# One block's k by a transposing load, its v on another queue, and PSUM copies placed by a table, in a two-layer H3 and SwiGLU kernel

## The chip, the cores and the metric

The kernel runs on one core of one Trainium2 chip. A core has five engines that run their own instruction streams and meet at semaphores: TensorE (PE in the profile; its weight loads are listed as PEld), VectorE (DVE), ScalarE (ACT), GpSimd (POOL) and SyncE (SP). DMAs are started by instructions on SP's and ACT's queues and carried out by 16 DMA engines. The metric is the device time of one execution in microseconds (us), lower is better.

## The reference

All arrays are bf16. Two equal layers run over x, a sequence of S = 2048 rows of D = 512 channels; the MLP has F = 1792 hidden channels. Both layers use the same q, k, v, filters and weights. Cut to what matters:

```python
def A(q, k, v, shift_k, ssm_k, ssm_D):            # H3: here q is LN(x)
    k_shift = sum(pad(k)[t:t+S] * shift_k[:, 3-t] for t in range(4))   # 4 taps per channel
    kv = k_shift * v
    y = irfft(rfft(kv, 2*S) * rfft(ssm_k, 2*S))[:S]    # causal convolution along S, per channel
    return q * (y + kv * ssm_D)
def B(x, w_gate, w_up, w_down):
    return (silu(x @ w_gate) * (x @ w_up)) @ w_down
x = A_q
for _ in range(2):
    x = x + A(layernorm(x), k, v, shift_k, ssm_k, ssm_D)
    x = x + B(layernorm(x), w_gate, w_up, w_down)
```

`k`, `v`, `shift_k`, `ssm_k` and `ssm_D` do not depend on x, so the convolution's result y is needed once and serves both layers.

## The kernel before, in words

**The convolution.** The 2048 rows are cut into four blocks of 512. Each block of kv and of the filter h (`ssm_k`) is turned into a spectrum by matmuls with cosine and sine tables (`fwd`), the spectra of two blocks are multiplied elementwise on DVE (`X` of kv by `G`/`H` of the filter, into `Z`), and matmuls with the transposed tables (`inv`) bring the products back (`Y`). The tables are made on the chip: iota on POOL, phases `ph` on DVE, Sin on ACT; `inv` is `fwd` through a transposing DMA. D is added to row 0 of the filter, once: `drow` is cleared by DVE, filled by a small DMA, and added by DVE when row 0 of h is copied out of PSUM (`transpose_h`, L479, the add at L502).

**The taps.** kv needs k shifted by 0 to 3 rows and scaled per channel. That is a matmul of k, transposed to channels by rows (`kTb`), against diagonal matrices `dg`: the identity times one tap, 16 of them (4 groups of channels by 4 taps). The taps come as `tapR`, are turned by PE into `tapF`, and the diagonals are made on DVE, ACT and POOL (L1188 and L1192). The result in PSUM is multiplied by v into `vt` (L536 for block 0).

**The first k.** For blocks 1 to 3, `kTb` is loaded by a transposing DMA (L366). For block 0 (`K0 = "rows"`) the rows are loaded plainly as `kn` (L364), `transpose_k` (L369 to L387) transposes them by 16 PE instructions (L378), and four copies bring them out of PSUM, two on ACT (L384) and two on DVE (L386).

**The FFN.** There are 16 units: layer by block by half a block of 256 rows. The normed rows are transposed to `zT`; gate and up projections go to PSUM tiles `pf` (matmuls of 256 columns, at the helper's line L323), Silu of the gate on ACT gives `sg` (L974), a copy of the up projection gives `ht` (L977, ACT), DVE multiplies them (L979), and the down projection goes to `pd` (L994), copied out as `dn` (L1075, ACT) and added to x. The layer norm's 1/sqrt is a power on POOL (`rstd`, L826, or L855 where ACT made the sums).

**The order of the work.** Every operation is recorded by `Plan.add` with an engine, a cost, the buffers it reads and writes, and perhaps a latency. `Plan.order` then sorts all operations by one table, `ORDER`, which was searched off the chip with these costs: `PW` and `PWA` are the costs of the two powers, `SAME` and `CROSS` the gaps between dependent operations of one or two engines. It gives PSUM slots (rings `pf` of 4, `pc` of 2, `pd` of 2) in that order, and each engine's instructions are issued in it. So the costs have no effect at run time except through the order and the slots. `Plan.issue` fills long planned gaps of PE before 32 us with dummy matmuls (`warm`, L1304).

**The queues at the start.** SP starts the loads of h of block 0 (`hn`), k, v, x (`xc`), h and v of block 1, the gate weights, then the two inverse tables, k of block 1, the up weights and the down weights. ACT's queue starts the taps and `drow`. PE runs 27 dummy matmuls, the taps' transposes, 16 transposes of h, then h spectrum and k transposes in turn, the 64 tap matmuls with h spectrum between, and from 13.6 us the spectrum of kv.

The lines that say what a sentence can't:

```python
def load_v(b, due=None, after=()):
    vt[b] = new("y" if b == 1 else "v", "vt", [P, R, D], parts=R)
    if b == 0 and K0 == "dma":
        return add("ACT", 0.45, lambda: nc.scalar.dma_start(out=vt[b].t[:], in_=v_t[:, b]), w=[vt[b]], lat=5.5, due=-69.5, after=[h0])
    return add("SP", 0.6, lambda: nc.sync.dma_start(out=vt[b].t[:], in_=v_t[:, b]), w=[vt[b]], ...)
```

Of the kernel before, what the change touches and what calls it, by code (L numbers as in the profile page):

```python
# [9 lines left out]
P = 128  # L10
# [13 lines left out]
PW = 1.2  # L24
# [15 lines left out]
DGE = 'DDAP'  # L40
# [3 lines left out]
PWA = 2.4  # L44
EVEN = True
SUMS = False
K0 = "rows"
CK0, LT0 = 3.0, 3.5
# [5 lines left out]
SHARE = {(1, 0, 1): 2, (0, 2, 0): 2, (1, 3, 0): 2}  # L54
ORDER = [
# [79 lines left out]


class Op:
    __slots__ = ("eng", "cost", "lat", "emit", "bufs", "preds", "succs", "due", "fixed", "conv", "grp", "dest", "sl", "end", "start", "n")


class Plan:
# [1199 lines left out]
```

## Time and profile before

| what | before |
|---|---|
| time, median of 3 runs (range) | 343.24 us (342.78 to 343.31) |
| the profiled execution: span, and with the 2.1 us around it | 341.1 us, 343.2 us |
| PE busy, matmuls | 336.9 us, 2563 |
| DVE busy, instructions | 282.4 us, 478 |
| ACT busy, instructions | 252.5 us, 496 |
| POOL busy, instructions | 37.3 us, 46 |
| share of PE in the chain that ended last | 94% |

How to read the profile. The span runs from the first to the last instruction of one profiled execution. The page gives busy time per engine, the span in 40 slices with the busy share of each in tenths, the chain of work that ended last, and groups of instructions by line. A row of a group is: line, engine, operation, output<-input, shapes, count | busy us, mean ns | idle us before them and what ended it. A row of the timeline is: start, duration, engine, line, operation, output<-input, shapes, count. A row of the chain is start, duration and what ran. The rows of the DMA view give KB of each and the median us from the issue to the landing; q1 is SP's queue there and q10 ACT's. Durations of a row of several matmuls include the last one's passage through the array.

### The profile page before, as it was taken

The numbers are of one execution on the slowest core, as the hardware profiler recorded it, in microseconds if no ns is written. First come the engines' busy times: TensorE is split into PE (matmuls) and PEld (weight loads), VectorE is DVE, ScalarE is ACT, GpSimd is POOL, SyncE is SP. The second block draws the span as 40 slices with busy tenths as digits, with TensorE's granted clock in tenths as the row PEclk, the third lists the DMA queues.
The fourth block names the chain that finished last, engine by engine and source line by source line (L and its number), as shares of the span: only waits on it lengthen the run. The fifth ranks groups of instructions, "written<-read, shape, count | busy, mean of one in ns | idle before, by whom it ended". The sixth has DMA issues, their size and how long they took to land.

```text
span 341.1 us, 6468 instructions
## 1 busy us (share of the span) xinstructions
PE 336.9 (99%) x2563; PEld 242.8 (71%) x2563; DVE 282.4 (83%) x478; ACT 252.5 (74%) x496; POOL 37.3 (11%) x46
## 2 busy tenths in 40 slices
PE   8999999999999999999999999999999999999996
PEld 7657858678687567768587756768685877777683
DVE  8899999999999999999999999889997533726022
ACT  7899999999977475778999973768665545545451
POOL 4000100002106100103100100101101000001000
PEclk9999999999999999999999999999999999999999
DMA  7999314050224175010110224010101110001111
GB/s 280 333 320 341 52 31 63 0 156 1 34 46 94 31 102 164 3 30 2 33 20 13 48 46 125 0 33 1 33 0 44 36 33 0 17 16 21 27 33 31
DMA packets 42088, 22.95 MB, mean 67 GB/s; under 512 B 33989, under 2 KB 39882, under 8 KB 42058
## 3 DMA queue, kind: packets, MB, share of 16 engines
q1 hardware_dynamic: 41904, 22.49, 26.0%
q8 instruction: 20, 0.33, 0.4%
q14 instruction: 10, 0.08, 0.1%
q10 hardware_dynamic: 154, 0.05, 0.1%
HBM read 12.33 MB, written 2.10 MB: 42 GB/s over the span
## 4 chain that ended last, share of the span: by engine, by line
PE 94%; ACT 3%; DMA 1%; SPq 0%; issue 0%; ACTq 0%
PE pf L323 57%; PE pd L994 28%; PE ps L323 6%; PE ps L470 2%; DMA kn<-in_A_k_dram 1%; ACT H L431 1%; ACT Yk L729 1%; ACT ks L526 0%; ACT n L874 0%; PE pt L378 0%; PE pt L489 0%; ACT zT L940 0%; ACT X L431 0%; SPq L354 0%; ACT xc L1052 0%
## 5 line engine op out<-in xcount | busy, mean ns | idle before, releaser
L323 PE MATMUL pf<-zT,wg_sb 128*128 128x256 bf16 (+1 forms) x872 | 110.3, 276 | 0.0
L323 PE MATMUL pf<-zT,wu_sb 128*128 128x256 bf16 (+1 forms) x872 | 110.0, 275 | 0.1
L994 PE MATMUL pd<-wd_sb,ht 128*128 128x512 bf16 (+1 forms) x462 | 106.2, 373 | 0.0
L323 PEld LDWEIGHTS <-wu_sb 128*128 128x128 bf16 x872 | 85.3, 98 | 18.9 <-issue 0.6
L323 PEld LDWEIGHTS <-wg_sb 128*128 128x128 bf16 x872 | 85.3, 98 | 17.3
L977 ACT CAST ht<-pf 128x512 bf16<-128x512 f32 x112 | 65.0, 592 | 23.0 <-PE pf L323 22.8
L974 ACT ACTIVATE sg<-pf 128x512 bf16<-128x512 f32 x112 | 66.6, 606 | 20.8 <-PE pf L323 17.3
L994 PEld LDWEIGHTS <-ht 128*128 128x128 bf16 x462 | 45.0, 98 | 44.1
L979 DVE TENSOR_TENSOR ht<-ht,sg 128x1024 bf16<-128x1024 bf16 (+1 forms) x61 | 38.9, 642 | 19.8 <-ACT ht L977 13.7
L826 POOL TENSOR_TENSOR rstd<-ve,nhalf 128x2 f32<-128x2 f32 x24 | 25.1, 1047 | 192.6 <-DVE ve L824 192.6
L821 DVE BATCH_NORM_STATS2 bnst<-xc 128x6 f32<-128x512 bf16 x48 | 31.8, 684 | 0.5
L1075 ACT CAST dn<-pd 128x512 bf16<-128x512 f32 x30 | 17.2, 590 | 17.5 <-PE pd L994 17.5
L431 ACT ACTIVATE X<-ps 128x512 bf16<-128x512 f32 x32 | 18.9, 606 | 10.5 <-PE ps L323 10.0
L1078 DVE TENSOR_TENSOR xc<-xc,dn 128x1024 bf16<-128x1024 bf16 x15 | 10.3, 687 | 16.8 <-ACT dn L1075 16.8
L669 DVE TENSOR_TENSOR t<-X,G 128x2048 bf16<-128x2048 bf16 x18 | 21.9, 1218 | 0.1
L665 DVE TENSOR_TENSOR t<-X,G 128x2048 bf16<-128x2048 bf16 x18 | 21.9, 1219 | 0.0
L855 POOL TENSOR_TENSOR rstd<-ve,nhalf 128x2 f32<-128x2 f32 x8 | 8.4, 1052 | 78.5 <-ACT ve L853 78.5
L679 DVE TENSOR_TENSOR Z<-Z,t 128x2048 bf16<-128x2048 bf16 x12 | 14.7, 1221 | 0.3
L677 DVE TENSOR_TENSOR t<-t,t 128x2048 bf16<-128x2048 bf16 x12 | 14.6, 1220 | 0.2
L431 ACT ACTIVATE H<-ps 128x512 bf16<-128x512 f32 x24 | 14.2, 612 | 0.0
L901 DVE TENSOR_TENSOR n<-n,Yk 128x1024 bf16<-128x1024 bf16 x15 | 10.3, 690 | 3.1 <-ACT n L874 1.9
L323 PE MATMUL ps<-hs,fwd 128*128 128x512 bf16 x40 | 12.7, 379 | 0.1
(103 smaller groups left out, 321.8 us busy)
## 6 DMA issues: line engine op xcount, KB each, us to landing
hn<-in_A_ssm_k_dram SPq DMA_DIRECT2D x4, 512.0 KB, 5.5
vt<-in_A_v_dram SPq DMA_DIRECT2D x4, 512.0 KB, 5.6
xc<-in_A_q_dram SPq DMA_DIRECT2D x4, 512.0 KB, 4.9
out_dram<-xc SPq DMA_DIRECT2D x15, 128.0 KB, 1.8
wg_sb<-in_B_w_gate_dram SPq DMA_DIRECT2D x1, 1792.0 KB
wu_sb<-in_B_w_up_dram SPq DMA_DIRECT2D x1, 1792.0 KB, 8.0
wd_sb<-in_B_w_down_dram SPq DMA_DIRECT2D x1, 1280.0 KB, 11.6
kn<-in_A_k_dram SPq DMA_DIRECT2D x1, 512.0 KB, 4.3
```

The costliest lines, as they stand in the source:

```text
L323: nc.tensor.matmul(o, lhsT=lhsT, rhs=rhs, start=(n == 0), stop=(n == len(terms) - 1))
L431: add("ACT", act(D), lambda: nc.scalar.activation(out=view(), in_=ps.t[:], func=ACT.Copy, scale=scale), r=[ps], w=[(buf, keys)], conv=conv)
L665: dve(n * D, lambda t1=t1, part=part: nc.vector.tensor_mul(out=t1.t[:], in0=x.t[:, sl, 0, :], in1=g.t[:, sl, part, :]), [(x, key(slots, (0 ...
L669: dve(n * D, lambda t2=t2, part=part: nc.vector.tensor_mul(out=t2.t[:], in0=x.t[:, sl, 1, :], in1=g.t[:, sl, 1 - part, :]), [(x, key(slots ...
L679: dve(n * D, lambda t1=t1, part=part: nc.vector.tensor_add(out=z.t[:, sl, part, :], in0=z.t[:, sl, part, :], in1=t1.t[:]), [t1], [zk], con ...
L821: add("DVE", 0.6, lambda st=st, i=i: nc.vector.bn_stats(out=st.t[:], in_=xs[c].t[:, i, :]), r=[(xs[c], (i,))], w=[st])
L826: add("POOL", pw, lambda: nc.gpsimd.tensor_tensor(out=rstd.t[:], in0=ve.t[:], in1=nhalf.t[:].to_broadcast((P, n)), op=ALU.pow), r=[ve, nha ...
L974: add("ACT", act(D), lambda ps=ps, sl=sl: nc.scalar.activation(out=sg.t[:, sl], in_=ps.t[:], func=ACT.Silu), r=[ps], w=[(sg, (b,))], due=( ...
L977: add("ACT", act(D), lambda ps=ps, sl=sl: nc.scalar.copy(out=ht.t[:, sl], in_=ps.t[:]), r=[ps], w=[(ht, (b,))], due=(us[0], at, 1.5, "a"))
L979: dve(n * m * W, lambda: nc.vector.tensor_mul(out=ht.t[:], in0=ht.t[:], in1=sg.t[:]), [sg], [ht], due=(us[0], (k + n) / NF, 0.0, "h"))
L994: nc.tensor.matmul((pds[o] if not cs.start else pds[HP]).t[:, cs], lhsT=ht.t[:, q, at, o * P:(o + 1) * P], rhs=wt["d"].t[:, ft, cs], start ...
L1075: add("ACT", act(D), lambda o=o: nc.scalar.copy(out=dn.t[:, o, :], in_=pds[o].t[:]), r=[pds[o]], w=[(dn, (o,))], due=(unit, 1.0, 3.0, "h"))
```

## The change

Block 0's k comes by the transposing load, straight into `kTb`, so `transpose_k` and its four copies are not called. In that mode the existing lines of `load_v` issue v of block 0 on ACT's queue, where it now stands between the taps and `drow`. SP starts h, k (transposing), x, h and v of block 1, the gate weights, and then as before. `Plan.add` gets an alternative engine for PSUM copies (`copy_out`) and for the tap diagonals; the table `FLIP` names which of these choices, counted in the order of recording, take the other engine. A copy on ACT is now an activation with Copy, one on DVE a `tensor_scalar`. Costs of the planner are changed, and `ORDER` is a new table of 1548 operations for 1556.

Counted over the program: PE loses the 16 transposes and two dummy matmuls and keeps all others. DVE loses two k copies and gets three more tap diagonals (11 for 8), 18 up-projection copies, four down-projection copies, two copies of inverse rows and the second of the first two `zT` copies. ACT loses two k copies, two diagonals (2 for 4) and the copies that go to DVE. POOL makes three diagonals for four. In the first FFN unit the gate projection comes first, before the up projection. One more output of block 2 is started by SP between the last outputs. At the start PE does the 16 h transposes (rows 3, 1, 0, 2), ten h-spectrum matmuls (rows 1 and 3 first), 36 tap matmuls, 2, 28 and 4 of these in turn, then v's spectrum. DVE, after the second diagonal and the copy of row 1 of h, waits for `drow`, adds it to row 0, makes nine diagonals and copies a spectrum.

```diff
-PW = 1.2
+PW = 0.69
...
-PWA = 2.4
+PWA = 0.69
...
+FIRST_ACT = True
-K0 = "rows"
-CK0, LT0 = 3.0, 3.5
+K0 = "dma"
+CK0, LT0 = 2.3, 3.9
...
+FLIP = {4, 5, 6, 9, 15, 17, 18, 19, 27, 49, 162, 163, 175, 183, 186, 209, 211, 213, 214, 217, 219, 222, 223, 225, 227, 230, 233, 234, 235, 236, 239, 240, 241, 242, 246}
 ORDER = [
-    0, 5, 1, 2, 3, 21, 16, 6, 14, 8, 15, 66, 69, 10, 7, 9, 4, 11, 34, 12, 17, 18, 13, 19, 20, 35, 26, 120, 121, 131, 27, 30, 31, 39, 37, 40, 36, 41,
...
+    8, 65, 5, 1, 0, 3, 13, 2, 12, 6, 38, 48, 10, 49, 14, 11, 4, 9, 15, 22, 20, 16, 17, 18, 23, 25, 26, 32, 51, 73, 91, 29, 36, 31, 35, 21, 30, 19,
...
-    SAME = {"PE": 0.0, "DVE": 0.12, "ACT": 0.05, "POOL": 0.1, "SP": 0.0}
-    CROSS = {"PE": 0.3, "DVE": 0.2, "ACT": 0.25, "POOL": 0.15, "SP": 0.0}
+    SAME = {"PE": 0.0, "DVE": 0.12, "ACT": 0.12, "POOL": 0.1, "SP": 0.0}
+    CROSS = {"PE": 0.2, "DVE": 0.14, "ACT": 0.15, "POOL": 0.05, "SP": 0.0}
...
+        o.alt = None
+        if alt is not None:
+            here, there = (eng, cost, emit), alt
+            if self.choices in FLIP:
+                here, there = there, here
+            self.choices += 1
+            (eng, cost, emit), o.alt = here, there
...
+    def copy_out(dst, src, r, w, eng="ACT", n=None, scale=1.0, cost=None, **kw):
+
+        n = n or D
+        costs = dict(cost or {"ACT": act(n), "DVE": tt1(n)})
+        forms = {"ACT": lambda: nc.scalar.activation(out=dst(), in_=src(), func=ACT.Copy, scale=scale),
+                 "DVE": lambda: nc.vector.tensor_scalar(out=dst(), in0=src(), scalar1=scale, scalar2=None, op0=ALU.mult)}
+        other = "DVE" if eng == "ACT" else "ACT"
+        return add(eng, costs[eng], forms[eng], r=r, w=w, alt=(other, costs[other], forms[other]), **kw)
...
-                    add("ACT", act(D), lambda ps=ps, sl=sl: nc.scalar.copy(out=ht.t[:, sl], in_=ps.t[:]),
-                        r=[ps], w=[(ht, (b,))], due=(us[0], at, 1.5, "a"))
+                    copy_out(lambda sl=sl: ht.t[:, sl], lambda ps=ps: ps.t[:].rearrange("p (b m w) -> p b m w", b=per, m=m),
+                             [ps], [(ht, (b,))], due=(us[0], at, 1.5, "a"))
...
+            e = {"D": "DVE", "A": "ACT", "P": "POOL"}[DGE[dt]]
+            other = {"DVE": "ACT", "ACT": "DVE", "POOL": "DVE"}[e]
+            add(e, *forms[e], r=[ident, tapF], w=w, alt=(other, *forms[other]))
```

More of the change, by code (lines that the diff above doesn't have):

```diff
@@ L155, in buf, with add @@
         return b
[L157 removed]
+    def add(self, eng, cost, emit, r=(), w=(), lat=None, due=None, conv=False, slack=0.0, after=(), dest=None, alt=None):
         o = Op()
+        o.alt = None
[5 more added lines that the diff above has]
+            (eng, cost, emit), o.alt = here, there
         o.eng, o.cost, o.emit, o.conv, o.n = eng, cost, emit, conv, len(self.ops)
@@ L382, in transpose_k @@
             src = lambda pt=pt: pt.t[:].rearrange("d r p -> d p r")
-            if engs[dt % len(engs)] == "ACT":
-                add("ACT", 0.47, lambda src=src, dst=dst: nc.scalar.copy(out=dst(), in_=src()), r=[pt], w=[(kT[b], (dt,))])
-            else:
-                add("DVE", tt1(D), lambda src=src, dst=dst: nc.vector.tensor_copy(out=dst(), in_=src()), r=[pt],
-                    w=[(kT[b], (dt,))])
+            copy_out(dst, src, [pt], [(kT[b], (dt,))], engs[dt % len(engs)], cost={"ACT": 0.47, "DVE": tt1(D)})
         return k_in
@@ L497, in transpose_h @@
             sl = slice(rows[0], rows[-1] + 1)
-            if engs[order.index(r0) % m] == "ACT":
-                add("ACT", act(len(rows) * D), lambda pt=pt, sl=sl: nc.scalar.copy(out=hs.t[:, sl, :], in_=pt.t[:]),
-                    r=[pt], w=[(hs, rows)], conv=conv)
-            elif row0 is not None and r0 == 0:
+            if row0 is not None and r0 == 0:
                 turns[0] = add("DVE", 0.335, lambda pt=pt: nc.vector.tensor_tensor(out=hs.t[:, 0, :], in0=pt.t[:, 0, :], in1=row0.t[:],
@@ L504, in transpose_h @@
             else:
-                turns[r0] = add("DVE", 0.335, lambda pt=pt, sl=sl: nc.vector.tensor_copy(out=hs.t[:, sl, :], in_=pt.t[:]),
-                    r=[pt], w=[(hs, rows)], conv=conv)
+                turns[r0] = copy_out(lambda sl=sl: hs.t[:, sl, :], lambda pt=pt: pt.t[:], [pt], [(hs, rows)], engs[order.index(r0) % m],
+                                     cost={"ACT": act(len(rows) * D), "DVE": tt2(len(rows) * D)}, conv=conv)
         return hs
@@ L606, in transpose_h_dma @@
         for r in range(R):
-            turned[b] = add("SP", 1.25, lambda r=r: nc.sync.dma_start_transpose(
-                out=hs.t[:, r].rearrange("p (k f) -> p k f", k=KD), in_=hr.t[:, r]), r=[hr], w=[(hs, (r,))], lat=3.0 if b == 1 else 1.9, conv=True)
+            turned[b] = add("SP", 1.22, lambda r=r: nc.sync.dma_start_transpose(
+                out=hs.t[:, r].rearrange("p (k f) -> p k f", k=KD), in_=hr.t[:, r]), r=[hr], w=[(hs, (r,))], lat=1.25, conv=True)
         return hs
@@ L623, in shift_mul_t @@
         for r in range(R):
-            add("SP", 1.25, lambda r=r: nc.sync.dma_start_transpose(
-                out=ks.t[:, 0, r], in_=a.t[:, 0, r]), r=[(a, range(KD))], w=[(c, (r,))], lat=4.0, conv=True)
+            add("SP", 1.22, lambda r=r: nc.sync.dma_start_transpose(
+                out=ks.t[:, 0, r], in_=a.t[:, 0, r]), r=[(a, range(KD))], w=[(c, (r,))], lat=1.25, conv=True)
         for h in range(2):
@@ L702, in inverse @@
                 r=[(z, key((r,))), inv], w=[ps], conv=True, dest=y)
-            add("ACT", act(D), lambda ps=ps, r=r: nc.scalar.copy(out=y.t[:, r, :], in_=ps.t[:]), r=[ps], w=[(y, (r,))],
-                conv=True)
+            copy_out(lambda r=r: y.t[:, r, :], lambda ps=ps: ps.t[:], [ps], [(y, (r,))], conv=True)
     def inverse_direct(k, slots_order):
@@ L724, with evacuate_y @@
     fresh = {}
-    def evacuate_y(k, rows):
+    def evacuate_y(k, rows, after=()):
         y, pss = Y[k], fresh[k]
         for r in rows:
-            add("ACT", act(D), lambda r=r: nc.scalar.activation(out=y.t[:, r, :], in_=pss[r].t[:], func=ACT.Copy, scale=2.0 if SUMS else 1.0),
-                r=[pss[r]], w=[(y, (r,))])
+            copy_out(lambda r=r: y.t[:, r, :], lambda r=r: pss[r].t[:], [pss[r]], [(y, (r,))], scale=2.0 if SUMS else 1.0, after=after)
     def inverse_rows(k):
@@ L886, in apply_norm @@
         rows = rows_of(h)
-        st = ln_stats_act(c, rows, after, (layer, c, h)) if on_act or ST1(layer, c, h) else ln_stats(c, rows)
-        nmr = shift_of(st, HP, due) if on_act or N_ACT(layer, c, h) else None
+        st = ln_stats_act(c, rows, after, (layer, c, h)) if on_act and FIRST_ACT or ST1(layer, c, h) else ln_stats(c, rows)
+        nmr = shift_of(st, HP, due) if on_act and FIRST_ACT or N_ACT(layer, c, h) else None
         n = new("n", "n", [P, HP, D], parts=HP)
@@ L936, in prologue @@
             pop = add("PE", pe(KD, P), go, r=[z, ident], w=[pt], due=-40)
-            if o:
-                add("DVE", 0.335, lambda pt=pt, o=o: nc.vector.tensor_copy(out=zT.t[:, :, o, :], in_=pt.t[:]), r=[pt], w=[(zT, (o,))], due=-45)
-            else:
-                add("ACT", act(D), lambda pt=pt, o=o: nc.scalar.copy(out=zT.t[:, :, o, :], in_=pt.t[:]), r=[pt], w=[(zT, (o,))], due=-45)
+            copy_out(lambda o=o: zT.t[:, :, o, :], lambda pt=pt: pt.t[:], [pt], [(zT, (o,))], "DVE" if o else "ACT",
+                     cost={"ACT": act(D), "DVE": tt2(D)}, due=-45)
             done = [zop, pop]
@@ L1074, in ffn @@
             for o in range(HP):
-                add("ACT", act(D), lambda o=o: nc.scalar.copy(out=dn.t[:, o, :], in_=pds[o].t[:]), r=[pds[o]], w=[(dn, (o,))],
-                    due=(unit, 1.0, 3.0, "h"))
+                copy_out(lambda o=o: dn.t[:, o, :], lambda o=o: pds[o].t[:], [pds[o]], [(dn, (o,))], due=(unit, 1.0, 3.0, "h"))
             sl = span(rows)
@@ L1186 @@
             w = [(dg, (dt * KS + j,))]
-            if DGE[dt] == "A":
-                add("ACT", 0.32, lambda j=j, dt=dt: nc.scalar.activation(out=dg.t[:, dt, j, :], in_=ident.t[:], func=ACT.Copy,
-                                                                        scale=tapF.t[:, dt, j:j + 1]), r=[ident, tapF], w=w)
-            else:
-                e, q, cost = ("POOL", nc.gpsimd, 0.57) if DGE[dt] == "P" else ("DVE", nc.vector, 0.163)
-                add(e, cost, lambda j=j, dt=dt, q=q: q.tensor_scalar(out=dg.t[:, dt, j, :], in0=ident.t[:],
-                                                                    scalar1=tapF.t[:, dt, j:j + 1], scalar2=None, op0=ALU.mult),
-                    r=[ident, tapF], w=w)
+            forms = {"ACT": (0.32, lambda j=j, dt=dt: nc.scalar.activation(out=dg.t[:, dt, j, :], in_=ident.t[:], func=ACT.Copy,
+                                                                            scale=tapF.t[:, dt, j:j + 1]))}
+            for e, q, cost in (("POOL", nc.gpsimd, 0.57), ("DVE", nc.vector, 0.163)):
+                forms[e] = (cost, lambda j=j, dt=dt, q=q: q.tensor_scalar(out=dg.t[:, dt, j, :], in0=ident.t[:],
+                                                                          scalar1=tapF.t[:, dt, j:j + 1], scalar2=None, op0=ALU.mult))
+            e = {"D": "DVE", "A": "ACT", "P": "POOL"}[DGE[dt]]
+            other = {"DVE": "ACT", "ACT": "DVE", "POOL": "DVE"}[e]
+            add(e, *forms[e], r=[ident, tapF], w=w, alt=(other, *forms[other]))
     k_in = transpose_k(0, "pc", eng(KTE)) if K0 == "rows" else k0
```

24 lines of the change are left out of this document (9 added, 15 removed), and 114 rows, old and new, of the table ORDER.

## The prediction

> **What bounds the kernel now.** I read the page first: the busy shares, the forty slices and the chain that ended last.
>
> ```profile
> span 341.1 us, 6468 instructions
> PE 336.9 (99%) x2563; PEld 242.8 (71%) x2563; DVE 282.4 (83%) x478; ACT 252.5 (74%) x496; POOL 37.3 (11%) x46
> ...
> DVE  8899999999999999999999999889997533726022
> ...
> PE 94%; ACT 3%; DMA 1%; SPq 0%; issue 0%; ACTq 0%
> ```
>
> TensorE (PE) is busy 99% of the span and carries 94% of the chain. The sum goes against this execution: its 341.1 us of span and the 2.1 us around it make 343.24, which is also the median of the runs shown. DVE is full until slice 29 (about 247 us) and loose behind it. Second, the busy time of each engine in four stretches, cut at the first transposition of h, the first v matmul, the first FFN matmul and the last PE work. Columns: PE, weight loads, DVE, ACT, POOL, granted clock, DMA share, GB/s.
>
> ```profile
> 4.35:13.56 9.21, 8.99 (x112) 7.02 (x113) 8.17 (x22) 8.24 (x21) 2.87 (x5) 1.00 1.03 388
> 13.56:32.23 18.67, 18.43 (x149) 10.85 (x148) 18.03 (x40) 18.17 (x37) 1.85 (x2) 1.00 1.08 321
> 32.23:338.17 305.94, 305.89 (x2269) 221.70 (x2268) 252.96 (x406) 223.87 (x438) 31.62 (x30) 1.00 0.19 40
> 338.17:341.10 2.93, 0.00 (x0) 0.00 (x0) 0.15 (x1) 0.31 (x1) 0.00 (x0) 1.00 0.23 68
> ```
>
> From 32.23 on PE is idle 0.05 us of 305.94, at full clock: with the same matmuls the order there can only hold the time or lose some. The tail is 2.93 us. What can be won lies ahead of 32.23, and there the second stretch has three engines at 96.6% or more. Third, the chain of waits and the timeline of that front (start, duration).
>
> ```profile
> 1.24 4.34 DMA kn<-in_A_k_dram
> ```
> ```profile
> 1.32 0.23 ACTq L1109 DMA_DIRECT2D drow<-in_A_ssm_D_dram  x1
> 1.78 0.42 SPq L394 DMA_DIRECT2D vt<-in_A_v_dram  x1
> 4.35 1.06 PE L489 MATMUL pt<-ident,hn 128*128 128x128 bf16 x16
> 5.14 0.41 DVE L502 TENSOR_TENSOR hs<-pt,drow 128x512 bf16<-128x512 bf16 x1
> 5.63 0.84 PE L378 MATMUL pt<-ident,kn 128*128 128x128 bf16 x12 [0.21 <-DMA kn<-in_A_k_dram]
> 6.31 1.03 PE L323 MATMUL ps<-hs,fwd 128*128 128x512 bf16 x4
> 9.79 3.07 PE L323 MATMUL ps<-dg,kTb 128*128 128x128 bf16 x52
> ```
>
> The chain ran over k: its plain load lands at 5.58, PE transposes it, and only then come the spectrum of h (6.31) and the tap matmuls.
>
> **The change, part by part.** *The 16 k transposes go.* For the pace of PE I need steady rows.
>
> ```profile
> 284.99 10.48 PE pf L323 x96
> 295.47 6.04 PE pd L994 x28
> ```
> ```profile
> 25.62 0.38 PE L323 MATMUL ps<-hs,fwd 128*128 128x512 bf16 x1
> ```
>
> 96 matmuls of 256 columns take 10.48, 0.109 each; 28 of 512 take 6.04, 0.216 each. One alone shows 0.38, so 0.164 of a row's last one is pipeline; the 52 tap matmuls of 128 columns are then (3.07 - 0.16) / 52 = 0.056 each. Sixteen k transposes are 0.90 of PE. With them goes the wait on k ahead of the h spectrum. In the new order PE does the 16 h transposes (to 5.26), then ten h-spectrum matmuls, 36 tap matmuls, 2 h, 28 tap, 4 h, then v's. The first of these needs only rows 1 and 3 of h, turned first: row 1 is out of PE by 4.35 + 8 x 0.056 + 0.16 = 4.96 and 0.41 of copy makes 5.37, so PE starts at about 5.4 and not 6.31. Sixteen matmuls of 512 and 64 of 128 are 3.45 + 3.58 = 7.03, so the first v matmul comes at about 12.45, 1.1 us earlier. This holds if three things arrive: k by 5.4 + 10 x 0.216 = 7.6, drow (the D row, added to row 0 of h) by 5.4 + 4 x 0.216 - 0.41 = 5.9, since the fifth of the ten reads row 0, and the tap diagonals from 7.6 on.
>
> *k by the transposing load.* The same instruction stands in this trace for block 1; beside it the plain loads (KB, us from issue to landing) and the rate while one ran.
>
> ```profile
> 16.09 2.33 SPq L366 DMA_TRANSPOSE kTb<-in_A_k_dram  x1
> ```
> ```profile
> hn<-in_A_ssm_k_dram SPq DMA_DIRECT2D x1, 512.0 KB, 3.6
> kn<-in_A_k_dram SPq DMA_DIRECT2D x1, 512.0 KB, 4.3
> vt<-in_A_v_dram SPq DMA_DIRECT2D x1, 512.0 KB, 5.6
> ...
> DMA packets 299, 0.40 MB, mean 402 GB/s; under 512 B 17, under 2 KB 262, under 8 KB 299
> q1 hardware_dynamic: 297, 0.40, 109.5%
> q10 hardware_dynamic: 2, 0.00, 0.3%
> ...
> DMA packets 3432, 0.89 MB, mean 254 GB/s; under 512 B 3423, under 2 KB 3423, under 8 KB 3432
> kTb<-in_A_k_dram SPq DMA_TRANSPOSE x1, 4.6
> ```
>
> Alone it lands 1.24 + 4.6 = 5.8. It follows h, which lands at 4.3, at 254 GB/s (2.1 us for 512 KB): 6.4 with nothing between. v is now issued on ScalarE's queue at about 1.3, right after the taps, while SP still needs 2.33 us to issue k; in order of arrival most of v goes first, 1.3 us at 402 GB/s, and k lands at about 7.7. That is the need of 7.6 to 0.1, so I take no delay; the ends are 5.8 (no delay) and 9.0 (h, v and x ahead of it, 1.4 late). The transfer costs 0.8 more of the DMA engines than the plain one, and SP reaches its next loads up to 1.9 later, less the 0.4 of v's issue: x, h1, v1, wg, inverse tables, k1, wu land about 1 us later.
>
> ```profile
> inv<-fwd SPq DMA_TRANSPOSE x1, 12.4
> ```
> ```profile
> 5.37 10.67 SPq L1198 DMA_TRANSPOSE inv<-fwd  x2
> ...
> 22.36 0.59 PE L809 MATMUL ps<-m,inv 128*128 128x512 bf16 x2
> 23.87 1.06 PE L323 MATMUL ps<-dg,kTb 128*128 128x128 bf16 x16
> ```
>
> The first inverse table landed 12.4 us after 5.37, at 17.8, and its first matmul ran at 22.36; k1 landed at 16.09 + 4.6 = 20.7 and was used at 23.87. With landing 1 later and use 1.1 earlier, 2.5 and 1.1 us of room are left, so they cost nothing; a further microsecond of lateness would be the first to show, on k1.
>
> *drow behind v.* Its queue now does taps, v, drow. In the stretch from 3 to 4 us above, q10 (ScalarE's queue) moved drow's packets, issued at 1.32, while q1 (SP's) moved 297 of h: they came only when h was nearly through, which looks like order of arrival over both queues. h and v together are the megabyte that h and k were, which landed at 5.58; drow then lands about 5.6 to 5.9, in time. Ends: 0, and 1.5 us late if k's pieces mix with v's. I take 0. Behind the waiting add on DVE stand nine tap diagonals and a spectrum copy, so a late drow also delays the taps.
>
> *The copies.* For the rest of the front the rows are these.
>
> ```profile
> 6.29 0.69 DVE L386 COPY kTb<-pt 128x512 bf16<-128x512 bf16 x1
> 6.50 0.58 ACT L384 COPY kTb<-pt 128x512 bf16<-128x512 bf16 x1
> 7.66 0.41 DVE L1192 TENSOR_SCALAR dg<-ident,tapF 128x128 bf16<-128x128 bf16 x2
> 31.28 0.42 DVE L938 COPY zT<-ptz 128x512 bf16<-128x512 bf16 x1
> 31.57 0.62 ACT L940 COPY zT<-ptz 128x512 bf16<-128x512 bf16 x1
> ```
>
> DVE loses two k copies (-1.38) and gains three diagonals (3 x 0.2 = 0.6): -0.78. ACT loses two k copies and two diagonals, about -1.9, and POOL one diagonal. The second zT copy goes from ACT, which ended 32.19, to DVE behind the first, 31.28 + 2 x 0.42 = 32.12: 0.07 better. DVE is what gains least and ends the wait for the first FFN matmul, so that moves from 32.23 by -0.85, to about 31.4; ends 0 (all lost in waits between the engines) and -1.1 (PE's whole gain).
>
> *Body and tail.* 18 copies of up-projections, four of down-projections and two of inverse rows go from ACT to DVE, at 0.69 for such a copy of f32 PSUM: 24 x 0.69 = 16.6 us.
>
> ```profile
> 8.03 0.69 DVE L434 TENSOR_SCALAR ev<-ps 128x512 bf16<-128x512 f32 x1
> ```
> ```profile
> 247.00:338.17 91.17, 91.13 (x687) 66.72 (x684) 44.27 (x89) 46.96 (x86) 5.15 (x7) 1.00 0.09 22
> ```
>
> All but three lie behind 247 us, where DVE is busy 44 of 91 us: hidden. If a DVE copy is late there, a PSUM buffer comes free late and PE waits. The planner's other costs (the rstd on POOL at 0.69 for 1.2 and 2.4) change only the order. I take 0 in the body; below nothing is excluded, since PE has 0.05 us of gaps there; above, see the third rival. One more output on SP in the tail fits ahead of the last: 0. Sum: 341.1 - 0.85 = 340.25, and 342.4 with the 2.1 around it.
>
> **The rivals.** *v takes half the DMA engines from h.* For it: both loads are posted by 1.7, before h's packets run at full rate. Against it: drow's packets above came late. Then h shares from the start and lands up to 1.1 later, about 5.4, where the megabyte ends at 5.58; everything behind follows: 342.4 + 1.1 = 343.5. [...] The trace's two late packets rather speak against it, without deciding.
>
> *k or drow lands late.* k at 8.4 to 9.0, or drow at 6.7 to 7.2, stops PE for 0.8 to 1.3 us in the front and takes back the gain: about 343.2. For it: k's need is met to 0.1 by my sum.
>
> *The body gets gaps (the other side).* rstd on POOL stands between each norm and its transposes.
>
> ```profile
> L826 POOL TENSOR_TENSOR rstd<-ve,nhalf 128x2 f32<-128x2 f32 x24 | 25.1, 1047 | 192.6 <-DVE ve L824 192.6
> ```
>
> The mean of the 24 is 1.05. The old order allowed 1.2 and 2.4, the new one 0.69, so one of mean length overruns its place by 0.36. With five of the 24 reaching PE the front's gain of 0.85 and the 0.69 that can be told are used up: (0.85 + 0.69) / 0.36 = 4.3. With six or seven it is 342.4 + 2.3 = 344.7 at most, 344.0 at five. Against it: sixteen units share the 306 us, 19 us each, and PE has other work in between.
>
> **How the numbers follow.** 0.2% is 0.69 us, about what a measurement tells from no change. Forecast 342.4, own range 341.5 to 342.9: chance 0.47 (0.41 faster, 0.06 within). Shared queues, 343.5: 0.17 (0.13 within, 0.04 slower). k or drow late, 343.2: 0.13 (0.03, 0.09, 0.01). Gaps in the body, 344.0 or more: 0.23 (0.01 within, 0.22 slower). That gives 0.44 faster, 0.29 within, 0.27 slower. The range is 341.4 to 344.3: it leaves out a larger gain in the second stretch (0.06) and the body's worse half (0.12).
>
> **What would show it.** Right: h lands at 4.3, the first h spectrum at 5.4, the first v matmul at 12.45, the first FFN matmul at 31.4, PE without gaps behind it, a tail of 2.9. Shared queues: h lands past 5. drow or k late: PE idle between 6.3 and 8 with that releaser. Body: PE busy under 305.9 of its stretch. Wrong altogether if the second stretch, with three full engines, does not pass on the earlier v.

## The result, and the profile after

The changed kernel takes 346.62 us (median of 6 runs, 346.4 to 348.5) against 343.24: a ratio of 1.0113, 95% interval 1.0092 to 1.0135. The forecast was 342.4. The profiled execution is the longest of the six; its span is 346.5 us, 2.0 less than its time.

From the page of the kernel after: span, busy time, the chain that ended last, and the group of the powers whose sums ACT makes.

```profile
span 346.5 us, 6452 instructions
...
PE 339.1 (98%) x2545; PEld 242.6 (70%) x2545; DVE 294.6 (85%) x504; ACT 236.6 (68%) x467; POOL 38.0 (11%) x45
...
PE 82%; ACT 8%; DVE 6%; POOL 2%; DMA 1%; issue 1%
...
L861 POOL TENSOR_TENSOR rstd<-ve,nhalf 128x2 f32<-128x2 f32 x8 | 11.5, 1437 | 66.8 <-ACT ve L859 66.8
```

PE's part of the chain fell from 94% to 82%; ACT, DVE and POOL came in. PE has 18 instructions fewer and is "busy" 2.2 us longer. The four stretches, cut at the same events as before (first h transposition, first v matmul, first FFN matmul, last PE work):

```profile
4.87:15.10 10.23, 10.23 (x96) 7.25 (x97) 7.03 (x20) 5.46 (x12) 1.41 (x4) 1.00 1.08 336
15.10:34.87 19.77, 18.52 (x148) 10.76 (x147) 18.01 (x41) 18.25 (x38) 3.50 (x2) 1.00 1.16 278
34.87:343.47 308.60, 306.66 (x2270) 221.35 (x2268) 266.06 (x430) 209.96 (x414) 31.61 (x30) 1.00 0.17 41
343.47:346.50 3.03, 0.00 (x0) 0.00 (x0) 0.19 (x1) 0.32 (x1) 0.00 (x0) 1.00 0.36 114
```

The first v matmul comes 1.54 later than before (15.10 for 13.56), the stretch behind it is 1.10 longer (19.77 for 18.67), the body 2.66 (308.60 for 305.94), the tail 0.10: together 5.40, the whole difference of the two spans. A second profile of the same kernel (below) has the first term at -0.40 and the others at +1.08, +2.63 and +0.09. So in these two the first term moves by 2 us and the others stay. The execution of the second profile took 346.48 us, close to the median of 346.62, so its terms are those of the measured difference.

The timeline of the front after (start, duration):

```profile
1.23 4.75 SPq L371 DMA_TRANSPOSE kTb<-in_A_k_dram  x1
...
4.87 1.89 PE L500 MATMUL pt<-ident,hn 128*128 128x128 bf16 x16 [0.41 <-DMA hn<-in_A_ssm_k_dram]
...
6.56 3.84 PE L334 MATMUL ps<-hs,fwd 128*128 128x512 bf16 x10
...
6.73 0.42 DVE L510 TENSOR_TENSOR hs<-pt,drow 128x512 bf16<-128x512 bf16 x1 [0.20 <-DMA drow<-in_A_ssm_D_dram]
...
10.23 2.17 PE L334 MATMUL ps<-dg,kTb 128*128 128x128 bf16 x36
```

and its DMA issues in the first 2 us (KB, us to landing):

```profile
hn<-in_A_ssm_k_dram SPq DMA_DIRECT2D x1, 512.0 KB, 4.1
vt<-in_A_v_dram ACTq DMA_DIRECT2D x1, 512.0 KB, 4.8
...
kTb<-in_A_k_dram SPq DMA_TRANSPOSE x1, 6.8
```

h lands at 4.8 and not 4.3, v at 6.1, drow not before 6.7, k at 8.0. The sixteen h transposes take 1.89 where they took 1.06, and the ten h-spectrum matmuls 3.84 where 10 x 0.216 + 0.16 = 2.32 was expected: PE runs them at half pace until 9.6. The page's granted clock stays at 1.00 (the last section says why).

In the body, the place where PE stands (columns as above):

```profile
61.23 1.22 DVE L673 TENSOR_TENSOR t<-X,G 128x2048 bf16<-128x2048 bf16 x1
61.26 3.47 POOL L861 TENSOR_TENSOR rstd<-ve,nhalf 128x2 f32<-128x2 f32 x1 [11.96 <-ACT ve L859]
62.36 0.69 DVE L983 TENSOR_TENSOR ht<-ht,sg 128x1024 bf16<-128x1024 bf16 x1
62.97 1.22 DVE L685 TENSOR_TENSOR t<-t,t 128x2048 bf16<-128x2048 bf16 x1
...
66.69 0.69 DVE L907 TENSOR_TENSOR n<-n,Yk 128x1024 bf16<-128x1024 bf16 x1 [2.50 <-ACT n L880]
```
```profile
67.19 0.38 PE L334 MATMUL ps<-hs,fwd 128*128 128x512 bf16 x1 [0.51 <-ACT H L440]
68.16 0.38 PE L334 MATMUL ps<-hs,fwd 128*128 128x512 bf16 x1 [0.59 <-ACT H L440]
73.98 1.25 PE L998 MATMUL pd<-wd_sb,ht 128*128 128x512 bf16 x5 [0.67 <-DVE ht L983]
```

One power on POOL takes 3.47 us while DVE runs products back to back; ACT's `n` and behind it ACT's PSUM copies wait for it, and PE for those. The chain that ended last (start, duration) leaves PE with this power and comes back to it 12.7 us later, through a second power, at the last of the three waits above:

```profile
61.26 3.48 POOL rstd L861
...
70.40 1.60 POOL rstd L832
72.02 0.16 DVE nmr L869
...
73.32 0.61 DVE ht L983
...
73.98 1.90 PE pd L998 x8
```

PE's waits in the body add up to 1.94 of the 2.66; the rest counts as busy. The same power in the kernel before:

```profile
58.97 0.88 POOL L855 TENSOR_TENSOR rstd<-ve,nhalf 128x2 f32<-128x2 f32 x1 [12.84 <-ACT ve L853]
```

### The profile page after: what moved, and what is told of

Its sections match the earlier page's. It is cut to its first block, busy times and chain, and to the rows that moved or that the text cites. A ratio compares the mean times of both kernels' runs of the same rounds, so it can differ in the third digit from the quotient of the medians.

```text
span 346.5 us, 6452 instructions
## 1 busy us (share of the span) xinstructions
PE 339.1 (98%) x2545; PEld 242.6 (70%) x2545; DVE 294.6 (85%) x504; ACT 236.6 (68%) x467; POOL 38.0 (11%) x45
## 4 chain that ended last, share of the span: by engine, by line
PE 82%; ACT 8%; DVE 6%; POOL 2%; DMA 1%; issue 1%
PE pf L334 49%; PE pd L998 25%; PE ps L334 6%; POOL rstd L861 2%; DMA hn<-in_A_ssm_k_dram 1%; ACT H L440 1%; ACT X L440 1%; ACT n L880 1%; PE ps L481 1%; ACT ht L440 1%; DVE ht L983 1%; DVE m L560 1%; DVE t L673 1%; DVE G L601 1%; ACT hr L611 1%
## 5 line engine op out<-in xcount | busy, mean ns | idle before, releaser
L978 ACT ACTIVATE sg<-pf 128x512 bf16<-128x512 f32 x112 | 65.8, 605 | 45.6 <-PE pf L334 44.6
L440 ACT ACTIVATE ht<-pf 128x512 bf16<-128x512 f32 x94 | 55.7, 608 | 21.4 <-PE pf L334 21.0
L832 POOL TENSOR_TENSOR rstd<-ve,nhalf 128x2 f32<-128x2 f32 x24 | 23.8, 1002 | 209.0 <-DVE ve L830 209.0
L440 ACT ACTIVATE dn<-pd 128x512 bf16<-128x512 f32 x26 | 15.4, 605 | 21.6 <-PE pd L998 21.6
L441 DVE TENSOR_SCALAR ht<-pf 128x512 bf16<-128x512 f32 x18 | 12.4, 688 | 11.7 <-PE pf L334 11.7
L673 DVE TENSOR_TENSOR t<-X,G 128x2048 bf16<-128x2048 bf16 x18 | 21.9, 1218 | 0.1
L861 POOL TENSOR_TENSOR rstd<-ve,nhalf 128x2 f32<-128x2 f32 x8 | 11.5, 1437 | 66.8 <-ACT ve L859 66.8
L334 PE MATMUL ps<-hs,fwd 128*128 128x512 bf16 x40 | 13.7, 424 | 1.1 <-ACT H L440 1.1
L685 DVE TENSOR_TENSOR t<-t,t 128x2048 bf16<-128x2048 bf16 x12 | 14.6, 1218 | 0.1
```

Of the source, the lines that this page charges most:

```text
L334: nc.tensor.matmul(o, lhsT=lhsT, rhs=rhs, start=(n == 0), stop=(n == len(terms) - 1))
L440: forms = {"ACT": lambda: nc.scalar.activation(out=dst(), in_=src(), func=ACT.Copy, scale=scale), "DVE": lambda: nc.vector.tensor_scalar(o ...
L673: dve(n * D, lambda t1=t1, part=part: nc.vector.tensor_mul(out=t1.t[:], in0=x.t[:, sl, 0, :], in1=g.t[:, sl, part, :]), [(x, key(slots, (0 ...
L685: dve(n * D, lambda t1=t1, t2=t2, comb=comb: nc.vector.tensor_tensor(out=t1.t[:], in0=t1.t[:], in1=t2.t[:], op=comb), [t2], [t1], conv=conv)
L832: add("POOL", pw, lambda: nc.gpsimd.tensor_tensor(out=rstd.t[:], in0=ve.t[:], in1=nhalf.t[:].to_broadcast((P, n)), op=ALU.pow), r=[ve, nha ...
L861: add("POOL", PWA, lambda: nc.gpsimd.tensor_tensor(out=rstd.t[:], in0=ve.t[:], in1=nhalf.t[:].to_broadcast((P, n)), op=ALU.pow), r=[ve, nh ...
```

## The experiments

Times are medians with their range, then the ratio to before with its 95% interval. Line numbers in the variants differ by a few. "Before" beside each was 343.0 to 343.3. Edits to `ORDER` are described by the operations moved.

**The kernel again**, unaltered.

> The changed kernel once more, unaltered. In its first profile TensorE did everything from 0.8 to 9.8 us at half pace (0.427 us per matmul of 512 columns for 0.216) and stood 2.7 us between 54 and 74 us. Theory A, the lowered clock at the start belongs to this kernel: half pace to about 9.8 us again, first FFN matmul at 34 to 35 us, time 346.4 to 347. Theory B, it is a matter of one execution: the ten h-spectrum matmuls at 0.216, and the time differs from run to run by 2 us or more. The stalls between 54 and 74 us hang on two long powers on GpSimd (3.5 and 1.6 us); I expect them to differ in size, 0.5 to 2.7 us.

345.66 (10 runs, 344.6 to 347.4; ratio 1.0053, 1.002 to 1.0087). Its profile has the ten h matmuls at full pace:

```profile
6.13 2.32 PE L327 MATMUL ps<-hs,fwd 128*128 128x512 bf16 x10
...
21.33 2.81 POOL L854 TENSOR_TENSOR rstd<-ve,nhalf 128x2 f32<-128x2 f32 x1 [15.04 <-ACT ve L852]
```
```profile
32.91:341.48 308.57, 306.64 (x2270) 221.32 (x2268) 266.00 (x430) 209.88 (x414) 31.57 (x30) 1.00 0.18 43
```

The first row is the ten h matmuls, the second the first power, the third the body's stretch. Theory B: the half pace is a matter of the execution. The body's stalls are not; I had expected them to vary, and they are the same to 0.03.

The same kernel is thus 3.4 us over before in one measurement and 2.3 in the other, and its executions spread from 344.6 to 348.5. A variant of it whose median lies 2.3 over before is not told from it by time; there the stretches of the profile have to speak.

**Dummies in the gap ahead of h.**

```diff
 def warm(ring, slot, n):
+    warms.append(n)
+    n = n + 6 if len(warms) == 2 else n
```

> The changed kernel with 9 dummy matmuls for 3 between the taps' transposes and the h transposes, so that TensorE does not stand 0.58 us before h lands at 4.82. Theory A1, the standing keeps the clock low: the clock is up at the latest by 6.4, the ten h-spectrum matmuls run at 0.216 for most, the first v matmul comes 1.5 to 2.9 us earlier than 15.1, time 343.7 to 345.3. Rival, the clock rises at moments that the dummies do not reach: half pace to 9.8 again and 346.6 (or 0.1 to 0.3 more, if the dummies hold h up).

346.47 (345.1 to 347.0; 1.0063, 1.0032 to 1.0095). No gain. In its profile PE is at full pace when h comes, 16 transposes in 1.05, and yet the first v matmul is at 13.30, no earlier than in the run above: PE now waits for row 0 of h, and that for drow. The fifth h matmul starts at 7.13, where 5.92 + 4 x 0.216 would be 6.78.

```profile
6.66 0.43 DVE L503 TENSOR_TENSOR hs<-pt,drow 128x512 bf16<-128x512 bf16 x1 [0.70 <-DMA drow<-in_A_ssm_D_dram]
...
7.13 1.46 PE L327 MATMUL ps<-hs,fwd 128*128 128x512 bf16 x6 [0.19 <-DVE hs L503]
```

**v on SyncE's queue behind k.**

```diff
-        return add("ACT", 0.45, lambda: nc.scalar.dma_start(out=vt[b].t[:], in_=v_t[:, b]), ...)
+        return add("SP", 0.45, lambda: nc.sync.dma_start(out=vt[b].t[:], in_=v_t[:, b]), ...)
```

> The changed kernel with v of block 0 on SyncE's queue behind k, so that nothing on ScalarE's queue runs beside h. Theory A2, v beside h is what makes h late: h lands at 4.3 to 4.4, TensorE stands less than 0.1 us, the clock is up as before the change, the h-spectrum matmuls start at about 5.4 at 0.216, v lands at 10 to 11 (needed at 12.3), time 343.5 to 344.5. Rival, the transposing load of k slows h down by itself: h lands at 4.7 to 4.9, half pace to 9.8, 346.6.

346.06 (344.5 to 346.9; 1.0062, 1.0033 to 1.0091): neither number, and no gain over the unaltered kernel's 345.66. h's transposes start at 4.58, 0.23 later than before, and ran at half pace in that execution (1.90 for 1.06). That k's transposing load holds h up is not shown: in a splice below with k by rows and v on SyncE's queue they start at 4.62, in a variant with the transposing load at 4.51. The first power stood as late here but was short, and the second stretch took 31.75 - 13.52 = 18.23 us:

```profile
21.70 1.19 POOL L854 TENSOR_TENSOR rstd<-ve,nhalf 128x2 f32<-128x2 f32 x1 [15.42 <-ACT ve L852]
```

**The kernel before without dummies** (each row of them cut to one).

> The kernel before, with each row of dummy matmuls cut to one (27, 3 and 2 become 1). Theory A, TensorE's pace at the start hangs on what it did in the microseconds before: half pace from 4.35 until at least 7.8, which is 64 or more column-hundreds lost, 1.5 to 3 us, time 344.7 to 346.2. Rival, the dummies are of no account: 343.2, h transposes at 0.056 each.

344.68 (343.8 to 346.5; 1.0034, 1.0004 to 1.0065): theory A's time, and in this profile its pace. The transposes took 1.90 from 4.37 (1.06 in the kernel before), the pace was half until about 9 (four h matmuls in 1.80 from 7.34 for 1.03; from 8.97 four k transposes in 0.39, as before), the first FFN matmul came 1.8 later.

**Splices at the first FFN matmul**: the front of the one kernel (order, engines, queues) and the body of the other.

> The changed kernel up to the first FFN matmul, and from there the order and the engines of the kernel before (the copies on ScalarE again). Theory O, the new order of the body stalls TensorE by itself: of the 2.7 us of gaps that the changed kernel shows between 50 and 75 us at most 0.3 are left, and the time falls by 2.4 to 2.7 against the changed kernel's, to 343 to 344. Rival F, the stalls are a debt of the front (ScalarE and DVE come out of it behind): gaps of 1 us or more stay between 33 and 75 us, time 345 to 346.

> The opposite: the kernel before up to the first FFN matmul (k by rows and TensorE, v on SyncE), then the changed kernel's order and engines. Theory O: the front as before (first FFN matmul at 32.2), gaps of 2.4 to 2.8 us about 31 to 39 us after it, a power on GpSimd of 3 us or more there, time 345.6 to 346. Rival F: no gaps, 343.2 to 343.5.

344.0 (342.7 to 346.0; 1.0023, 1.0001 to 1.0046) and 346.57 (346.4 to 347.0; 1.0087, 1.0072 to 1.0102). The bodies, first that of before behind the new front, then that of after behind the old one:

```profile
33.32:339.40 306.08, 304.50 (x2241) 221.56 (x2268) 253.11 (x406) 223.79 (x438) 31.06 (x30) 1.00 0.19 42
```
```profile
32.60:341.70 309.10, 305.26 (x2241) 221.35 (x2268) 265.80 (x430) 210.10 (x414) 31.94 (x30) 1.00 0.17 41
```

(Some matmul records are missing in both, so their PE busy time is short; the lengths are not.) Theory O: the body's 2.5 to 3.2 us go with the new order of the body, whatever front it has.

**k by the transposing load alone**, in the order and on the engines of before, with v behind it on SyncE's queue. (The source is the changed one with `FLIP` empty, so the PSUM copies have their new forms.)

```diff
-K0 = "rows"
+K0 = "dma"
```

> The kernel before in its own order, with one part of the change alone: k of block 0 by the transposing load, v behind it on SyncE's queue. By the prediction's sum TensorE saves 0.9 us and the wait on k ahead of the h spectrum goes, so the first FFN matmul comes 0.5 to 0.9 earlier than 32.2 and the time is 342.3 to 342.8. Rival: the transposing load's long issue holds v until 6 us, v lands at 10 to 10.5 and the first product by v waits, or h lands 0.2 to 0.3 late beside it and the clock rises late: 343.2 to 344.

342.53 (7 runs, 342.2 to 343.0; 0.9971, 0.996 to 0.9982): faster than both kernels. As forecast, this part is a gain, of 0.8 at the median.

**The new front with v on SyncE's queue, and the body of before.**

> The changed kernel's front with v on SyncE's queue behind k, and the body of the kernel before. With the front of that variant as measured (first FFN matmul at 31.75) and a body without gaps (305.9), a tail of 2.9 and 2.1 around the span: 342.7; 342.4 to 343.4 over executions whose clock rises at different moments. If the body's stalls are a debt of the front: 344.5 or more.

343.54 (342.1 to 344.1; 1.0004, 0.9991 to 1.0017). In its profile the first power took 2.81 again, as in the run of the kernel again, and the first FFN matmul came at 32.63 and not 31.75. The searched front is 1.0 slower than the old one with k's load changed: its second stretch took 32.63 - 12.88 = 19.75 us, that of the old one 32.33 - 13.55 = 18.78.

**v on ScalarE's queue, alone.** The first variant left v where the order table had it, far back in that queue:

> The kernel before with k of block 0 by the transposing load and, as the changed kernel has it, v of block 0 on ScalarE's queue ahead of drow; order and engines of before. It differs from the run with v on SyncE's queue (342.53) by that queue alone. Theory Q, v beside h costs: h lands 0.2 to 0.5 later than there, drow at 6.4 to 6.7 instead of 5.2, and TensorE stands before row 0 of h: 343.0 to 344.5. Rival, the queue is of no account: 342.3 to 342.7.

349.24 (347.8 to 350.4; 1.0177, 1.0148 to 1.0207). This doesn't answer the question: v was issued at 6.36, behind x, h, v and gate weights of later use, and the first product by v waited until 15.21.

```profile
6.36 0.36 ACTq L393 DMA_DIRECT2D vt<-in_A_v_dram  x1
...
15.21 0.69 DVE L537 TENSOR_TENSOR vt<-ps,vt 128x512 bf16<-128x512 f32 x1 [6.54 <-DMA vt<-in_A_v_dram]
```

The second has v between the taps and drow:

> The kernel before with k by the transposing load and v on ScalarE's queue between the taps and drow, as in the changed kernel (in the run before this one v stood far back in that queue, at 6.4 us). Against the same with v on SyncE's queue (342.53). Theory Q, the queue costs: drow lands at 6.4 to 6.7 and k at 7.6 to 8.0 instead of 6.3, TensorE stands 0.5 to 1.5 us before row 0 of h or the first taps, 343.2 to 344.2. Rival, no cost: 342.3 to 342.8.

343.56 (343.4 to 345.3; 1.0016, 1.0001 to 1.003), 1.0 more than with v on SyncE's queue. Theory Q. What PE waits for is drow, which stands behind v in that queue; v on ScalarE's queue behind drow was not tried. Row 0 of h there, with its wait and PE's, and the same row with v on SyncE's queue:

```profile
6.56 0.42 DVE L503 TENSOR_TENSOR hs<-pt,drow 128x512 bf16<-128x512 bf16 x1 [1.32 <-DMA drow<-in_A_ssm_D_dram]
7.04 0.94 PE L327 MATMUL ps<-hs,fwd 128*128 128x512 bf16 x3 [1.23 <-DVE hs L503]
```
```profile
5.22 0.42 DVE L503 TENSOR_TENSOR hs<-pt,drow 128x512 bf16<-128x512 bf16 x1
```

**The power in the body.** In the changed kernel two DVE products (t1 at L673, and L685) are moved from beside the power to behind the next statistics.

```diff
 ORDER:  ... rstd (POOL) | t2 | 
-        t1 (L673) | ht | t (L685) | n | xc | bn_stats x2 | bn_aggr x2 | ht | ve | Z ...
+        ht | n | xc | bn_stats x2 | bn_aggr x2 | ht | ve | t1 (L673) | t (L685) | Z ...
```

> The changed kernel with two of DVE's elementwise products of 2048 columns moved from beside GpSimd's power at 59 to 61 us (3.48 us long) to behind the next statistics, where the following power runs (1.60 us). Theory L, the power waits while DVE runs products of two SBUF operands back to back: the first power falls to 0.7 to 1.2 and the gaps of 1.4 us at 64 to 66 us go; the second power grows to 3 us or more and TensorE's gap at 71 us grows with it. Rival, the powers have their own lengths at those places (cold code, the operands): 3.5 and 1.6 as before and the same gaps.

> The changed kernel with the two DVE products moved away from GpSimd's power, timed (one look gave 343.98, with the clock up early and a short first power). Its body shows 1.87 us of gaps for 2.72, so against the changed kernel under like conditions 0.8 to 0.9 less: median 344.7 to 345.9.

A single execution took 343.98; four others 345.67 (344.4 to 345.8; 1.0072, 1.0054 to 1.009), in the range given, but 2.4 over before like the unaltered kernel. What shows the effect is the body, 307.7 us in the profiles of both measurements for 308.6. The power and DVE in the single execution, and its body:

```profile
57.67 0.69 POOL L854 TENSOR_TENSOR rstd<-ve,nhalf 128x2 f32<-128x2 f32 x1 [11.95 <-ACT ve L852]
58.59 0.69 DVE L976 TENSOR_TENSOR ht<-ht,sg 128x1024 bf16<-128x1024 bf16 x1 [0.87 <-ACT ht L433]
...
64.06 1.59 POOL L825 TENSOR_TENSOR rstd<-ve,nhalf 128x2 f32<-128x2 f32 x1 [5.71 <-DVE ve L823]
```
```profile
31.28:339.00 307.72, 306.30 (x2270) 221.41 (x2268) 266.11 (x430) 210.05 (x414) 28.85 (x30) 1.00 0.18 43
```

The power falls from 3.47 to 0.69 and PE's two waits for `H` (0.51 and 0.59) go: theory L. The following power didn't grow, against my expectation (1.59 in both); PE's wait behind it grew from 0.67 to 1.25, because the moved products now stand ahead of the `ht` that PE waits for. Net 0.85 of 2.66.

**The first power.** ACT's last statistics step `ve` and the power, moved up to where the sums are ready.

```diff
 ORDER, ScalarE:  ... Square (sums ready) |
-  X | X | hs | X | hs | X | ve (then rstd on POOL) | X | H ...
+  ve (then rstd on POOL) | X | X | hs | X | hs | X | X | H ...
```

> The changed kernel with ScalarE's last statistics step of the first norm, and with it GpSimd's power, issued as soon as the sums are there (about 19.2 us) and not behind nine PSUM copies (22.9 in the first profile). Theory E, that late start and the 2.8 us of the power make the gap of 1.09 us at 27 to 29 us: the gap goes, the first FFN matmul comes 1.0 to 1.4 earlier against its first v matmul (18.4 to 18.8 behind it and not 19.8), the time falls by about 1 us to 345 to 345.7. Rival, the gap comes from ScalarE's load as a whole: it stays at 0.8 or more.

345.35 (345.0 to 346.6; 1.0075, 1.0057 to 1.0092), again 2.3 over before. The power starts at 17.90 and takes 0.80, and the first FFN matmul follows the first v matmul by 32.01 - 13.34 = 18.67 us, as in the kernel before, where the changed kernel had 19.77 and 19.75. Theory E, by the stretch. The first power in the kernel before, in the first profile after, and here:

```profile
16.41 1.15 POOL L855 TENSOR_TENSOR rstd<-ve,nhalf 128x2 f32<-128x2 f32 x1 [9.12 <-ACT ve L853]
```
```profile
23.29 2.80 POOL L861 TENSOR_TENSOR rstd<-ve,nhalf 128x2 f32<-128x2 f32 x1 [17.01 <-ACT ve L859]
```
```profile
17.90 0.80 POOL L854 TENSOR_TENSOR rstd<-ve,nhalf 128x2 f32<-128x2 f32 x1 [11.60 <-ACT ve L852]
```

**Three repairs at once**: v on SyncE's queue, the early first power, the moved products.

> The changed kernel with three repairs at once: v on SyncE's queue behind k, the first norm's statistics step and power issued early, the two DVE products moved. If the causes add (0 to 0.5 for the queue, about 1.1 for the late first power, 0.85 for the power in the body), 346.6 falls by 2 to 2.5, to 344.1 to 344.6 at the median, with 1.8 to 1.9 us of gaps left in the body, none over 0.6 us between the first v matmul and the first FFN matmul; 343.3 or less in executions whose clock rises early. If they do not add: 345 or more.

344.38 (6 runs, 344.2 to 344.6; 1.0034, 1.0022 to 1.0047). All six lie below all sixteen of the unaltered kernel (344.6 to 348.5), so the three together are a gain in time, of 1.3 or 2.2 by which of its two medians is taken; 2 to 2.5 was expected. The second stretch is 18.67 again and the body 307.7, and the 2.7 us of spread between executions shrink to 0.4. What is left of PE's waits in the body is, but for 0.16, one of its order:

```profile
70.10 1.90 PE L991 MATMUL pd<-wd_sb,ht 128*128 128x512 bf16 x7 [1.25 <-DVE ht L976]
```

**More dummies in the best variant.**

> The variant with k by the transposing load alone (342.53), with six dummy matmuls for three ahead of the h transposes, against the 0.28 us that TensorE stands there. If standing keeps the clock low in some executions: 341.9 to 342.4 and less spread. If the moment of the clock's rise is not reached by so little: 342.5 as before, or 0.1 more.

342.64 (11 runs, 342.2 to 343.1; 0.9987, 0.9978 to 0.9996): no gain over 342.53 (0.4 below before here, 0.8 there). In its profile six dummies took 0.61 from 3.95 and the transposes 1.05, the first v matmul came at 12.76, 0.8 earlier than before, and the first FFN matmul at 31.54; in that of the other variant the transposes took 1.90, and it was at 32.33, in the longest of its seven runs.

## Why the prediction was wrong, by its own steps

The span of the second profile is 344.5 us where 340.25 was forecast. By the forecast's own marks (12.45, 31.4) that is 0.71 at the first v matmul, 0.80 in the second stretch, 2.63 in the body and 0.09 in the tail. The largest step that failed is the body at 0.

**k's transposes go, and the wait on k.** Right, and shown alone: -0.8 of the time, and in the profile with more dummies a first v matmul 0.8 earlier. The 0.85 of the forecast was for the whole new front, so that the two agree so closely is in part chance. The new front has the gain too; other steps took it back.

**k by the transposing load lands at 7.7, no delay.** 7.5 to 8.0 over the profiles, and no delay, since the taps came later still. The issue took 4.3 to 4.75 us of SyncE with v on ScalarE's queue and 3.0 to 3.2 with v behind it, and not the 2.33 of the row I had used.

**drow behind v, "5.6 to 5.9, in time", cost 0.** Wrong: over the profiles with v ahead of drow the add of row 0 began at 6.2 to 6.7, against a need of 5.9. It is a term mis-sized by 0.3 to 0.8, and the prediction had its end (1.5 late) but took the other. In the new front it cost PE 0.35 (7.13 for 6.78, with nine dummies); where PE ran at half pace it was hidden. In the old order, which needs row 0 sooner, v ahead of drow costs 1.0.

**v shares the DMA engines with h.** A rival at 343.5. Half right: h landed at 4.1 to 4.8 over the profiles with v on ScalarE's queue, at 4.3 to 4.5 in those with v on SyncE's, so at the worst 0.3 to 0.5 late, and not 1.1. The rival had h share from the start, but v, issued at 1.31, moved its first packets at 3.7 in the first profile after. In the DMA view there, from 4 to 5 us (packets, MB, share of the engines), v's queue q10 had nearly all of the engines' time; q1 had the end of h, and k waited:

```profile
q10 hardware_dynamic: 94, 0.39, 93.6%
q1 hardware_dynamic: 30, 0.03, 7.7%
```

By the packets that the trace lists, from 3.8 to 4.4 us, while both queues had some, q10 moved 50 and q1 61. But v's packets are of 4 KB (0.39 MB in 94) and h's of 1 KB (0.03 MB in 30), so these like counts gave v four times the bytes, 0.20 MB for 0.05. Of k's packets, which are under 512 bytes, 4 moved from 4 to 5 us and 554 from 5 to 6, though k was issued at 1.23. Up to 4 us 16 packets under 512 bytes had moved; with k alone and v behind it on SyncE's queue it was 162.

**The pace of 0.216 per matmul from 5.4 on.** An unstated condition of the walk: the rows I took it from lie at 25 us and later. In the first profile after, PE ran at half pace until 9.6. The sixteen transposes and ten matmuls lost 0.83 + 1.52 us by it there (1.89 and 3.84 for 1.06 and 2.32). Of the 1.94 by which the first term moves between the two profiles, the ten matmuls make 1.51, h's later start (4.87 for 4.51) 0.36 and the way from one to the other 0.07.

**The second stretch passes on what DVE gains.** Wrong by 1.1, and no rival named it. I counted the instructions that move between engines and not the place of those that stay: the new order puts ACT's `ve` of the first norm behind more PSUM copies, so its power ran at 23.3 where it ran at 16.4, with no room for 2.8 us. This step was missing. The late place alone is not the cost: with the power at that place the stretch is 19.75 to 19.77 us in the five profiles where the power took 2.8, and 18.23 in the three where it took 1.2, which is 0.44 less than before.

**The body at 0.** Wrong by 2.66, the largest term. The third rival had the mechanism, the power on POOL, and the sign, at a chance of 0.23, but its price was a mean: 0.36 for each power and five of 24 needed. (Five times 0.36 is 1.8, so its 344.0 should have read 344.2.) In fact the chain puts PE's waits behind one power of 3.47 and the 1.6 that follows, and the long one is of the other kind (L861, after sums on ACT) whose row I hadn't quoted. The moved products show 0.85 of the 2.66. That the rest belongs to the new order is shown by the splices; that it hangs on the second power is read from the chain and was not tested. Most of the other powers cost nothing, and length alone is no price: the longest of all stands in the kernel before, whose PE is idle 0.05 us in the whole body.

```profile
105.56 6.21 POOL L826 TENSOR_TENSOR rstd<-ve,nhalf 128x2 f32<-128x2 f32 x1 [11.57 <-DVE ve L824]
```

The mean hid that one power took 0.69 or 3.47 by what DVE did beside it, and that its price is set by who waits for it. The copies moved to DVE late in the kernel were hidden, as forecast, and so was the extra output (tail 3.03).

Why the power grows: it was 0.69 with DVE idle and 3.47 beside three products, and the moved products settle that. Three long ones end 0.54 to 0.58 us after the first moment at which DVE has nothing running: at 64.73 (DVE done at 64.19), at 24.14 in the second profile (DVE pauses from 23.56 to 23.60), at 111.77 in the kernel before (111.22 to 111.26). The 0.88 of the kernel before had products on both sides, with such a pause at 59.31, 0.54 ahead of its end. The first of the three ran on through three products and ended 0.54 us after the last. By what DVE holds the power up was not shown.

## What to carry to other kernels

Before pricing a new order, list for each short operation on GpSimd what VectorE runs beside it: a mean duration says little when it is 0.7 or 3.5 by its neighbours. Then ask what waits for it: 6.2 us cost nothing where nothing did. Look at what an order moves and not only at what a diff adds, above all single small steps that a long chain hangs on. And when one part of a bundled change is sound (here the transposing load), run that part alone: it was 0.8 us faster while the bundle was 2.3 to 3.4 us slower.

## What the runs showed of the hardware that was not expected

TensorE's half pace at the start ends at very different moments: by 4 us in the profile before (three dummies in 0.34 from 3.95, for 0.50 in the two of the changed kernel) and in the one with nine dummies (these in 0.70 from 3.95), about 5.5 in the unaltered kernel's second profile (16 transposes in 1.52 from 4.51), 9.6 in its first, about 9 without dummies. It shows in the durations (16 transposes: 1.05 or 1.9). It is the granted clock, though the page gives 1.00: the traces hold records of this clock, and the first one, at full, begins at 3.73 in the kernel before and at 9.62 in the first profile after, where the pace doubles. The time ahead of it has no record, and the views count it as full. In the run with v far back in ScalarE's queue, where PE stood 1.40 us for v, the pace was half once more in the middle: 28 dummies took 1.81 from 12.75, eleven 1.38 from 20.28, and the granted clock of that profile is 0.995.

The moments differ by 6 us over the profiles. PE waited 0.41 us for h in the execution that stayed slow longest, but 0.28 in a variant (k's load changed, v on ScalarE's queue ahead of drow) whose transposes, from 4.73, took 1.08. What decides between executions stays open.

The first power took 2.81 or 1.20 us in executions where the DVE instructions around it were the same, at the same distances to 0.01 us: it ended at 22.43, before DVE's next three products, or at 24.14, after them. These are the two rows, from the kernel run again and from the single execution with moved products:

```profile
21.33 2.81 POOL L854 TENSOR_TENSOR rstd<-ve,nhalf 128x2 f32<-128x2 f32 x1 [15.04 <-ACT ve L852]
```
```profile
21.23 1.20 POOL L854 TENSOR_TENSOR rstd<-ve,nhalf 128x2 f32<-128x2 f32 x1 [14.96 <-ACT ve L852]
```

Up to 57 us the two kernels issue the same instructions, so what was issued up to there does not set the length alone. It is worth 1.5 us of the second stretch (19.75 for 18.23). No kernel shows both lengths in its own profiles (2.8 twice in the changed kernel, 1.20 twice in the variant), so what decides stays open.
